# Attention into a top-1 mixture of experts: two comparisons in one piece, kept tokens' slots on GpSimd, eleven filler matmuls instead of twenty

## The chip, the cores and the metric

The kernel runs on one core of a Trainium2 chip. The metric is the device time of one execution in microseconds (us), median of three runs. The engines of the core are named as the profile names them: PE (TensorE matmuls; PEld are its weight loads), DVE (VectorE), ACT (ScalarE), POOL (GpSimd) and SP (SyncE, which here only issues DMAs). Each engine works through its own instructions in the order in which the program holds them, and waits for the others on semaphores.

## What is computed

Attention over 4 batches, 8 heads, 768 positions and a head size of 64, with 4 sink positions and a window of 128; its output, 3072 tokens of 512 numbers, goes into a layer of 8 experts. Each token goes to the expert of its largest logit, each expert keeps at most 80 tokens (those with the largest gate weight), and all other tokens give zero rows.

```python
scores = np.where(is_sink | in_window, scores / 8, -1e9)
a = softmax(scores); x = (a @ v) as (3072, 512)
logits = x @ w_gate                      # (3072, 8)
expert_idx = np.argmax(logits, axis=1); gate_w = softmax(logits)[chosen]
for e in range(8):
    tok = tokens of e; if len(tok) > 80: keep the 80 with the largest gate_w
    out[tok] = gate_w[tok, None] * (np.maximum(x[tok] @ w1[e], 0.0) @ w2[e])
```

## The kernel before

**Stages.** The 3072 tokens are 24 tiles of 128. The main loop goes through attention in 48 ticks (`scores`, `softmax`, `exps`, `transposes`, `weighted`, `keep_x`). Behind it, in the shadow of the following ticks, come the token rows (`rows_turn`, `rows_keep`, `rows_scale`, `rows_write`, which writes them to `x_rows` in DRAM), the gate (`gate_products` to `gate_keys`) and the ranking. After the loop a piece of code written out by hand ends attention for the last four tiles (`g0` = 20 to `i` = 23), and finishes the ranking. Then the selection (`rank`, `hot`, `pi`, `idx_in`) makes the list of token numbers per expert, and the expert stage gathers the tokens' rows from `x_rows` by these numbers (`gather`, an indirect DMA on POOL's queue), transposes them (`tokens`, the tile `px`) and runs two matrix products per expert (`ffn1`, `ffn2`).

**Ranking.** A token's key is a number that orders by expert and gate weight. Tile i's tokens are compared with all tokens before them: `rank_compare` runs on DVE over a row of all keys, `krow`, in pieces of up to `PIECE` = 768 columns. A piece that ends in tile i itself is a SCALAR_TENSOR_TENSOR with the table `ties` as a second tensor, any other one a TENSOR_SCALAR; both add up along the row. At tile `CUT` = 16 the first 2048 tokens are thinned to at most 80 per expert, so later tiles compare from column 2048 on (`C0`), and with the 640 kept keys (`kept_row`, piece number `NPC - 1`). Tiles 22 and 23 have 896 and 1024 columns of their own: two pieces each, 0 and 1. PE counts the results by column (`rank_count`, `rank_count_last`).

**Kept tokens.** `kept_rank` (80 x 8) is where the kept tokens stand after all, and `kept_hots` (80 x 8 x 80) their one-hot slots. DVE makes them in one TENSOR_TENSOR. PE multiplies them with `kept_picks` into `pi`, and behind that the `hot` of the last eight tiles with `picks`. ACT copies `lanes` out of `pi`, DVE makes `idxf`, POOL `idx_in`.

**Order.** From the loop to the end of the ranking the order on every engine is that of the code (`manual_schedule`). In the selection this holds for DVE and POOL, in the expert stage for all. SP issues weights (`load_weight`, 1 MB in four DMAs) and token rows in one queue, in program order.

**Fillers.** `warm(n)` issues n matmuls of no use on PE. Between the selection and the expert stage 20 more such matmuls (`warm1`, 480 columns each) stand on PE ahead of the first `tokens`.

Of the kernel before, what the change touches and what calls it, by code (L numbers as in the profile page):

```python
# [243 lines left out]
def attention_moe(ctx: ExitStack, tc, q, k, v, n_sink, window, w_gate, w1, w2, capacity, q_t, k_t, v_t, vs_t, wg_t, out):  # L244
# [28 lines left out]
    picks = const.tile([P, NTILE, 5, E], BF16, name="picks")  # L273
    PIECE, NPC, NGT = 768, 4, 6
    CUT = 16
# [52 lines left out]
    with ExitStack() as actx:  # L328
# [136 lines left out]
        po.memset(negc, NEG)  # L465
        ties = const.tile([P, PIECE], BF16, name="ties")
        e_down = const.tile([P, E], F32, name="e_down")
# [24 lines left out]
        def make_ties():  # L492
            po.memset(ties, TINY)
            po.affine_select(out=ties[:, PIECE - P:], in_=ties[:, PIECE - P:], pattern=[[-1, P]],
                             compare_op=ALU.is_gt, fill=0.0, base=0, channel_multiplier=1)
# [96 lines left out]
        def transposes(t):  # L592
            prob = st[(t, "p")]
            pp = ps_p.tile([P, 2, 2, P], F32, tag="pp", name=f"pp_{t}")
            for a in range(2):
                for h in range(2):
                    pe.transpose(pp[:, a, h], prob[:, a, h, SINK:], ident)  # L597
            st[(t, "pp")] = pp
# [5 lines left out]
        def sinks_keep(t):  # L604
            ac.copy(stt_rows[t % 2][0:SROWS].bitcast(F32R), ts_bank)
# [192 lines left out]
        def keys_keep(i0, nb):  # L798
            ac.copy(krow[:, i0 * P:(i0 + nb) * P], gst.pop((i0, "pk"))[:, 0:nb * P])
            for i in range(i0, i0 + nb):  # L800
                lo = 0 if i < CUT else C0
                todo = [(i, n, c, min(c + PIECE, (i + 1) * P)) for n, c in enumerate(range(lo, (i + 1) * P, PIECE))]
                if i >= CUT and i0 > CUT:
                    todo.append((i, NPC - 1, None, None))
                rank_todo.extend(todo)
            if i0 == CUT:
                rank_todo.extend((i, NPC - 1, None, None) for i in range(i0, i0 + nb))
# [3 lines left out]
        def rank_compare():  # L811
            i, n, c0, c1 = rank_todo.pop(0)
            gt = wk.tile([P, PIECE], BF16, tag="gt", name=f"gt_{i}_{n}", bufs=NGT)
            ra = parts[:, i, n:n + 1]
            if c0 is None:
                ve.tensor_scalar(gt[:, 0:E * CAP], kept_row, keys[:, i:i + 1], None, ALU.is_ge, ALU.add, accum_out=ra)
                rank_done.append((None, None, gt))
                return
            w = c1 - c0
            if c1 == (i + 1) * P:  # L820
                ve.scalar_tensor_tensor(gt[:, 0:w], krow[:, c0:c1], keys[:, i:i + 1], ties[:, PIECE - w:],
                                        ALU.subtract, ALU.is_gt, accum_out=ra)
            else:
                ve.tensor_scalar(gt[:, 0:w], krow[:, c0:c1], keys[:, i:i + 1], None, ALU.is_ge, ALU.add,
                                 accum_out=ra)
            if min(i * P, c1) > c0:
                rank_done.append((c0, min(i * P, c1), gt))
# [240 lines left out]
        with tc.manual_schedule():  # L1068
# [65 lines left out]
            sink_probs(t)  # L1134
            transposes(t)
            keep_probs(t)
            weighted(t - 1)
            keep_x(t - 1)
            rows_scale(g0, 0)
            rows_write(g0, 0, nc.sync)  # L1140
            own_probs(t)
            before_probs(t)
            assert not rank_todo, rank_todo
            recip(i, 1)
            keys_turn(g0, 2)
            keys_keep(g0, 2)
            sinks_turn(t)
            sinks_keep(t)
            compare(g0, NPC - 1)
# [12 lines left out]
            keep_x(t)  # L1162
            for _ in range(2):
                load_weight()
            rows_turn(g0, 1)
            gate_products(i, 1)
            rows_turn(i - 1, 0)
            rows_keep_scaled(g0, 1, "xr")
            rows_write(g0, 1, nc.sync)
            gate_logits(i, 1)  # L1170
            keys_turn(i - 1, 1)
# [16 lines left out]
            rank_count()  # L1188
            for n in (NPC - 1, 0, 1):
                compare(i - 1, n)  # L1190
# [20 lines left out]
            for c in range(E // 2):  # L1211
# [11 lines left out]
            kept_hots = const.tile([CAP, E, CAP], BF16, name="kept_hots")  # L1223
            ve.tensor_tensor(kept_hots, slot_row[0:CAP, None, :].to_broadcast([CAP, E, CAP]),
                             kept_rank[:, :, None].to_broadcast([CAP, E, CAP]), ALU.is_equal)
            in_row = {}
            for j in range(CUT, NTILE - 1):
                in_row.setdefault(j // NM, []).append(j % NM)
            for r, ms in in_row.items():
                j0, j1 = r * NM + ms[0], r * NM + ms[-1] + 1  # L1230
                ve.tensor_tensor(colacc[:, j0:j1], colacc[:, j0:j1],
                                 ct[:, 0:c0].rearrange("p (m k) -> p k m", k=rows)[:, r, ms[0]:ms[-1] + 1], ALU.subtract)
            warm(3)
            compare(i, 1)
            rank_count_last(more)
            warm(3)
# [3 lines left out]
    with ExitStack() as fctx:  # L1240
# [40 lines left out]
        with ExitStack() as wctx:  # L1281
            wps = wctx.enter_context(tc.tile_pool(name="ps_warm", bufs=1, space=PSUM))
            wt = wps.tile([P, 512], F32, name="warm1")
            for _ in range(20):
                pe.matmul(wt[0:CAP, 0:480], hot[:, NNEW - 1], hot[:, 0:6].rearrange("p t c -> p (t c)"), start=True, stop=True)
# [198 lines left out]
```

## Time and profile before

| | |
|---|---|
| median of three runs | 297.01 us (296.69 to 297.58) |
| profiled execution, its own time | 295.55 us |
| its span, first to last instruction | 293.8 us |
| busy: PE, DVE, ACT, POOL | 94%, 58%, 56%, 55% of the span |
| last tick's scores, start of the hand-written end | about 179 us |
| expert stage, first transpose to last matmul on PE | 206.3 to 287.9 us |
| mean granted TensorE clock | 0.983 |

A row of the timeline gives the start in us from the span's start, the duration in us (of the whole group where several equal instructions were merged, `x20`), the engine, the line of the kernel, the operation, what it writes and reads, the shapes, and in brackets the idle time of the engine ahead of it and who ended that wait. `SPq` is SP issuing a DMA. A table of stretches gives each engine's busy us, the granted clock (`PEclk`, 1.00 is 2.4 GHz and 0.50 is 1.2 GHz) and the DMA share.

### The profile page before, as it was taken

To read this page: it belongs to the slowest core of one execution; us is meant where nothing else is said; L and a number is where in the kernel's file an instruction comes from. 1 tells how busy PE (TensorE), PEld (TensorE's weight loads), DVE (VectorE), ACT (ScalarE), POOL (GpSimd) and SP (SyncE) were. 2 spreads that over 40 slices of the span, in tenths; PEclk is the share of its full clock that TensorE was granted. 3 is DMA by queue.
4 is the path that set the end of the run, shared out by engine and by line. 5 is a ranking of instruction groups with operands and counts; after the bars stand their busy time and mean duration, and the time that the engine had idled before them with its cause. 6 is when DMAs were issued, how large, how long until landed. Compare 5 with 4: busy or idle time off the path is not lost. (4 is left out here: it accounts for less than half of the span.)

```text
span 293.8 us, 10499 instructions
## 1 busy us (share of the span) xinstructions
PE 277.6 (94%) x4015; PEld 218.0 (74%) x4015; DVE 169.4 (58%) x564; ACT 165.1 (56%) x670; POOL 160.6 (55%) x365
## 2 busy tenths in 40 slices
PE   7989999999999999999999999988999999999991
PEld 2666777667777677777668777644999999999980
DVE  6678868767888979989996897990000000000001
ACT  4867888878887878687678778630112122212210
POOL 5966978658988768769757686735211121011111
PEclk9999999999999999999999999995999999999997
DMA  6989570899560999764174915595999999999501
GB/s 173 381 281 367 220 284 6 291 280 325 198 243 32 288 340 407 269 207 146 49 284 138 353 50 170 166 317 193 322 315 297 310 278 321 325 291 305 206 26 34
DMA packets 33364, 69.71 MB, mean 237 GB/s; under 512 B 4251, under 2 KB 6427, under 8 KB 32923
## 3 DMA queue, kind: packets, MB, share of 16 engines
q1 hardware_dynamic: 32282, 66.34, 66.6%
q0 software_dynamic: 1024, 2.62, 3.0%
q8 instruction: 34, 0.56, 0.8%
q14 instruction: 24, 0.19, 0.2%
HBM read 55.05 MB, written 13.89 MB: 235 GB/s over the span
## 5 line engine op out<-in xcount | busy, mean ns | idle before, releaser
L581 ACT ACTIVATE prob<-sc,nm 128x132 f32<-128x132 f32 (+1 forms) x192 | 68.9, 376 | 8.0 <-DVE nm L571 7.8
L544 PE MATMUL sc<-kv,q 64*128 64x260 f32 (+1 forms) x384 | 57.6, 401 | 5.1 <-ACT prob L581 3.7
L544 PEld LDWEIGHTS sc<-kv,q 64*128 64x128 f32 x384 | 30.1, 185 | 25.1 <-ACT prob L581 15.3
L609 ACT COPY pt<-pp 128x512 f32<-128x512 f32 x48 | 28.1, 585 | 32.4 <-PE pp L597 27.0
L571 DVE TENSOR_REDUCE nm<-sc 128x2 f32<-128x264 f32 (+1 forms) x96 | 41.3, 431 | 3.3
L564 DVE COPY_PREDICATED sc<-upper,sc 128x256 f32<-128x256 int8 x80 | 33.7, 422 | 15.8 <-PE sc L544 10.8
L581 ACT ACTIVATION_READ_ACCUMULATOR prob<-sc,nm 128x1 f32 x192 | 40.6, 211 | 0.0
L638 PE MATMUL xp<-pt,kv 128*64 128x128 f32 x384 | 37.0, 285 | 0.0
L1335 DVE COPY xs<-px 128x320 f32<-128x320 f32 x7 | 3.4, 491 | 56.3 <-PE px L1330 49.5
L617 POOL TENSOR_SCALAR_AFFINE_SELECT own<-pt 128x512 f32<-128x512 f32 (+1 forms) x48 | 27.2, 566 | 15.6 <-ACT pt L609 14.3
L1404 POOL DMA_INDIRECT out_dram<-y,idx x8 | 7.4, 925 | 46.1 <-ACT y L1398 42.0
L597 PEld LDWEIGHTS pp<-ident,prob 128*128 128x128 f32 x192 | 20.2, 141 | 15.9 <-issue 10.5
L597 PE MATMUL pp<-ident,prob 128*128 128x128 f32 x192 | 31.4, 286 | 0.0
L638 PE MATMUL xp<-own,kv 128*64 128x128 f32 x320 | 31.1, 273 | 0.0
L624 POOL TENSOR_SCALAR_AFFINE_SELECT pt<-pt 128x512 f32<-128x512 f32 (+1 forms) x48 | 28.3, 589 | 3.3
L688 POOL TENSOR_TENSOR xr<-xr,rs 128x512 f32<-128x512 f32 x21 | 22.4, 1067 | 6.7 <-ACT xr L676 6.4
L1352 PE MATMUL ph<-xs,w 128*64 128x80 f32 x640 | 25.6, 233 | 0.1
L1370 PE MATMUL py<-h,w 128*64 128x80 f32 x640 | 24.8, 234 | 0.6 <-ACT yt L1381 0.6
L1370 PEld LDWEIGHTS py<-h,w 128*64 128x64 f32 x640 | 23.1, 137 | 1.6 <-issue 0.8
L1352 PEld LDWEIGHTS ph<-xs,w 128*64 128x64 f32 x640 | 23.6, 137 | 0.4 <-DVE xs L1332 0.3
L638 PEld LDWEIGHTS xp<-pt,kv 128*64 128x64 f32 x384 | 21.1, 136 | 3.5 <-POOL pt L624 0.2
L1356 ACT ACTIVATE h<-ph 128x320 f32<-128x320 f32 x16 | 7.0, 437 | 29.3 <-PE ph L1352 29.3
(193 smaller groups left out, 523.0 us busy)
## 6 DMA issues: line engine op xcount, KB each, us to landing
w<-in_moe_w_dram SPq DMA_DIRECT2D x80, 256.0 KB, 4.7
kv_w<-in_moe_w_dram SPq DMA_DIRECT2D x48, 256.0 KB, 4.3
kv<-in_v_t_dram SPq DMA_DIRECT2D x12, 512.0 KB
out_dram<-zeros SPq DMA_DIRECT2D x24, 256.0 KB, 2.5
x_rows<-xr SPq DMA_DIRECT2D x24, 256.0 KB, 2.1
q<-in_q_t_dram SPq DMA_DIRECT2D x11, 512.0 KB, 5.7
kv<-in_k_t_dram SPq DMA_DIRECT2D x3, 1584.0 KB, 8.4
kv<-in_k_t_dram SPq DMA_DIRECT2D x2, 528.0 KB, 6.3
```

The lines of the kernel that those rows point to most:

```text
L544: pe.matmul(sc[:, h, c0:c0 + w], qs[g][r, hp, j % 2 * P:(j % 2 + 1) * P], ks[b][r, hp, k0:k0 + w], start=True, stop=True)
L564: ve.copy_predicated(own, upper, sc[:, :, 0:P])
L571: ve.tensor_reduce(out=nm, in_=sc[:, :, lo_c:hi_c], axis=AX.X, op=ALU.max, negate=True)
L581: ac.activation(prob[:, a, h, p0:], sc[:, h, lo_c:hi_c], AF.Exp, bias=nm[:, h:h + 1], scale=1.0, accum_out=ssum[:, n, 2 * hp + h:2 * hp + ...
L597: pe.transpose(pp[:, a, h], prob[:, a, h, SINK:], ident)
L609: ac.copy(pt, st.pop((t, "pp")))
L617: po.affine_select(out=own[:, a0:], in_=pt[:, a0:], pattern=[[0, 2 - a0], [0, 2], [1, P]], compare_op=ALU.is_ge, fill=0.0, base=0, channel ...
L624: po.affine_select(out=pt[:, a0:], in_=pt[:, a0:], pattern=[[0, 2 - a0], [0, 2], [-1, P]], compare_op=ALU.is_gt, fill=0.0, base=0, channel ...
L638: pe.matmul(xp[h * D:(h + 1) * D, a * P:(a + 1) * P], val[:, (2 * hp + h) * D:(2 * hp + h + 1) * D], pr[:, a, h], start=False, stop=(a == ...
L688: po.tensor_tensor(xr, xr, gst[(i0, "rs")][:, n, :, None].to_broadcast([P, H, D]), ALU.mult)
L1352: pe.matmul(ph[m * D:(m + 1) * D, f], columns(0, e, c, fc * P + m * D), x[:, c], start=(c == 0 and not (wide and f)), stop=(c == DC - 1), ...
L1370: pe.matmul(to[m * D:(m + 1) * D, dc], columns(1, e, k, dc * P + m * D), h[:, k], start=(k == 0), stop=(k == HC - 1), skip_group_check=True)
```

## The change

Six edits, all but the first in the hand-written end.

1. Pieces of tiles 16 and up may have 1024 columns (`WHOLE`): tiles 22 and 23 are compared in one SCALAR_TENSOR_TENSOR each. `ties` grows to 1024 columns, and two result tiles `gtw` are added. One `warm(3)` between the two old pieces of tile 23 goes.
2. `kept_hots` is made on POOL, in eight TENSOR_SCALARs of 80 x 80, one per expert.
3. For the last tick, POOL does the two selections of probabilities (`own_probs`, `before_probs`) ahead of scaling the rows of tile 20 (`rows_scale`), and the write of these rows follows later.
4. The transpose of the last tick's sink columns (`sinks_turn`) and its copy (`sinks_keep`) come earlier on PE and ACT.
5. Of two loads of weights in a row, the second is issued behind the write of tile 21's rows.
6. The 20 fillers ahead of the expert stage become 11.

```diff
-    PIECE, NPC, NGT = 768, 4, 6
+    PIECE, NPC, NGT, WHOLE = 768, 4, 6, 1024
...
-        ties = const.tile([P, PIECE], BF16, name="ties")
+        ties = const.tile([P, WHOLE], BF16, name="ties")
...
+                width = WHOLE if i >= CUT else PIECE
+                todo = [(i, n, c, min(c + width, (i + 1) * P)) for n, c in enumerate(range(lo, (i + 1) * P, width))]
...
-            gt = wk.tile([P, PIECE], BF16, tag="gt", name=f"gt_{i}_{n}", bufs=NGT)
+            if c0 is not None and c1 - c0 > PIECE:
+                gt = wk.tile([P, WHOLE], BF16, tag="gtw", name=f"gt_{i}_{n}", bufs=2)
+            else:
+                gt = wk.tile([P, PIECE], BF16, tag="gt", name=f"gt_{i}_{n}", bufs=NGT)
...
             transposes(t)
+            sinks_turn(t)
             keep_probs(t)
+            sinks_keep(t)
             weighted(t - 1)
             keep_x(t - 1)
+            own_probs(t)
+            before_probs(t)
             rows_scale(g0, 0)
             rows_write(g0, 0, nc.sync)
-            own_probs(t)
-            before_probs(t)
...
-            sinks_turn(t)
-            sinks_keep(t)
...
-            for _ in range(2):
-                load_weight()
+            load_weight()
             rows_turn(g0, 1)
             gate_products(i, 1)
             rows_turn(i - 1, 0)
             rows_keep_scaled(g0, 1, "xr")
             rows_write(g0, 1, nc.sync)
+            load_weight()
...
-            for n in (NPC - 1, 0, 1):
+            for n in (NPC - 1, 0):
                 compare(i - 1, n)
...
-            ve.tensor_tensor(kept_hots, slot_row[0:CAP, None, :].to_broadcast([CAP, E, CAP]),
-                             kept_rank[:, :, None].to_broadcast([CAP, E, CAP]), ALU.is_equal)
+            for e in range(E):
+                po.tensor_scalar(kept_hots[:, e], slot_row[0:CAP], kept_rank[:, e:e + 1], 1.0, ALU.is_equal, ALU.mult)
...
-            warm(3)
-            compare(i, 1)
-            rank_count_last(more)
             warm(3)
             ve.tensor_tensor(colacc[:, CUT:i], colacc[:, CUT:i], more[:, 0:i - CUT], ALU.subtract)
...
-            for _ in range(20):
+            for _ in range(11):
                 pe.matmul(wt[0:CAP, 0:480], hot[:, NNEW - 1], hot[:, 0:6].rearrange("p t c -> p (t c)"), start=True, stop=True)
```

DVE at the end of the ranking, before: the comparisons of tiles 22 (`gt_0_3434`, `gt_1_3436`) and 23 (`gt_0_3482`, `gt_1_3505`), the kept tokens' slots and the last `hot`.

```order
L824 TENSOR_SCALAR gt_0_3434,parts<-krow,keys 128x768
L821 SCALAR_TENSOR_TENSOR gt_1_3436,parts<-krow,keys,ties 128x128
L816 TENSOR_SCALAR gt_3_3463,parts<-kept_row,keys 128x640
L824 TENSOR_SCALAR gt_0_3482,parts<-krow,keys 128x768
L1216 TENSOR_REDUCE os<-ot 128x8
L1221 TENSOR_TENSOR kept_rank<-kept_rank,ct 80x8
L1222 TENSOR_TENSOR kept_rank<-kept_rank,last 80x8
L1224 TENSOR_TENSOR kept_hots<-slot_row,kept_rank 80x640
L1231 TENSOR_TENSOR parts<-parts,ct 128x2
...
L821 SCALAR_TENSOR_TENSOR gt_1_3505,parts<-krow,keys,ties 128x256
L1237 TENSOR_TENSOR parts<-parts,more 128x7
L1255 TENSOR_REDUCE rank<-parts 128x8
```

DVE at the same place, after the change:

```order
L825 SCALAR_TENSOR_TENSOR gt_0_3434,parts<-krow,keys,ties 128x896
L820 TENSOR_SCALAR gt_3_3461,parts<-kept_row,keys 128x640
L825 SCALAR_TENSOR_TENSOR gt_0_3480,parts<-krow,keys,ties 128x1024
L1220 TENSOR_REDUCE os<-ot 128x8
L1225 TENSOR_TENSOR kept_rank<-kept_rank,ct 80x8
L1226 TENSOR_TENSOR kept_rank<-kept_rank,last 80x8
L1235 TENSOR_TENSOR parts<-parts,ct 128x2
...
L1238 TENSOR_TENSOR parts<-parts,more 128x7
L1256 TENSOR_REDUCE rank<-parts 128x8
L1264 TENSOR_TENSOR hot<-slot_row,rank 128x320 x2
```

Two operations with one tensor became two with two tensors, the last piece of tile 23 moved ahead of `os`, and `kept_hots` left DVE.

POOL from the end of the ranking to the first gather, after the change (`off` and `ot` lead to `os` and `kept_rank`, `xg` takes the gathered rows); before, the row of `kept_hots` is not there and all others stand in the same order.

```order
L1203 TENSOR_TENSOR off<-off,kept_ahead 128x8
L1205 TENSOR_TENSOR ot<-onehot,off 128x64
L1207 TENSOR_TENSOR kept_rank<-kept_slot,off 80x8
L1221 TENSOR_TENSOR parts<-later,os 128x8
L1229 TENSOR_SCALAR kept_hots<-slot_row,kept_rank 80x80 x8
L1252 MEMSET xg_3529 1x1
...
L1276 TENSOR_SCALAR idx_in<-idxf 80x8
L1292 DMA xg_3529<-x_rows,idx_in 80x512
```

Eight instructions now stand between POOL's last sum and its making of the token numbers.

SP's queue over the last rows and weights, before:

```order
L692 DMA x_rows<-xr_0_3197 128x512
L317 DMA kv_w_3312<-in_moe_w_dram 128x512 x8
L692 DMA x_rows<-xr_1_3340 128x512
L692 DMA x_rows<-xr_0_3369 128x512
L692 DMA x_rows<-xr_0_3410 128x512
L317 DMA kv_w_3312<-in_moe_w_dram 128x512 x4
```

and after the change:

```order
L692 DMA x_rows<-xr_0_3197 128x512
L317 DMA kv_w_3312<-in_moe_w_dram 128x512 x4
L692 DMA x_rows<-xr_1_3336 128x512
L317 DMA kv_w_3312<-in_moe_w_dram 128x512 x4
L692 DMA x_rows<-xr_0_3369 128x512
L692 DMA x_rows<-xr_0_3410 128x512
L317 DMA kv_w_3312<-in_moe_w_dram 128x512 x4
```

Ahead of the last write of rows (`xr_0_3410`, tile 23) stand the same transfers as before; only tile 21's rows (`xr_1`) moved in between the weights.

## Rows read from the trace of the kernel before

**Rows 1.** Table of stretches: five engines' busy us, PEclk, DMA share, GB/s.

```profile
199.30:205.00 5.70, 5.69 (x15) 2.69 (x15) 0.00 (x0) 0.00 (x0) 3.82 (x8) 0.50 0.44 148
205.00:205.50 0.50, 0.50 (x4) 0.20 (x3) 0.00 (x0) 0.00 (x0) 0.00 (x0) 0.72 1.11 295
...
206.30:281.00 74.70, 74.07 (x1977) 71.66 (x1975) 3.68 (x8) 14.32 (x30) 10.39 (x11) 1.00 0.89 291
```

**Rows 2.** Timeline from the selection to the first transpose: start, duration, engine, what.

```profile
197.89 0.64 PE L1266 MATMUL pi<-picks,hot 128*80 128x40 bf16 x8
...
199.15 0.28 POOL L1275 TENSOR_SCALAR idx_in<-idxf 80x8 int32<-80x8 f32 x1 [3.00 <-DVE idxf L1274]
199.31 7.14 PE L1285 MATMUL warm<-hot 128*80 128x480 bf16 x20 [0.78 <-ACT tab L1278]
...
200.66 1.22 POOL L1291 DMA_INDIRECT xg<-x_rows,idx_in  x1 [1.23 <-DMA x_rows<-xr]
...
206.29 0.44 PE L1330 MATMUL px<-ident,xg 80*128 80x80 f32 x4
```

**Rows 3.** View of the tile xg, first gather alone: us from its start to landing.

```profile
DMA to landing us min/median/max: 3.3/3.3/3.3
```

**Rows 4.** View of x_rows, last write (tile 23) alone: durations, first and last start.

```profile
L692 SPq DMA_DIRECT2D x_rows<-xr x1: 319/319/319, 193.0 to 193.0; - x1
...
DMA to landing us min/median/max: 6.7/6.7/6.7
```

**Rows 5.** View of the tile w, the last six DMAs of weights.

```profile
L317 SPq DMA_DIRECT2D w<-in_moe_w_dram x6: 328/328/338, 268.9 to 273.0; - x6
...
DMA to landing us min/median/max: 4.5/4.5/4.5
```

**Rows 6.** Timeline of PE, start of the last expert's second product.

```profile
281.16 1.33 PE L1370 MATMUL py<-h,w 128*64 128x80 f32 x32 [0.58 <-ACT yt L1381]
```

**Rows 7.** Timeline of DVE at the end of the ranking.

```profile
193.49 1.01 DVE L824 TENSOR_SCALAR_CACHE_REDUCE gt<-krow,keys 128x768 bf16<-128x768 f32 x1
...
194.42 0.21 DVE L1216 TENSOR_REDUCE os<-ot 128x8 f32<-128x64 f32 x1
...
195.02 0.82 DVE L1224 TENSOR_TENSOR kept_hots<-slot_row,kept_rank 80x640 bf16<-80x640 f32 x1
...
195.96 0.47 DVE L821 SCALAR_TENSOR_TENSOR gt<-krow,keys,ties 128x256 bf16<-128x256 f32 x1
...
197.25 0.89 DVE L1263 TENSOR_TENSOR hot<-slot_row,rank 128x320 bf16<-128x320 f32 x2
```

**Rows 8.** Timeline of DVE and POOL: one POOL operation twice, beside different DVE operations.

```profile
186.22 0.88 DVE L821 SCALAR_TENSOR_TENSOR gt<-krow,keys,ties 128x640 bf16<-128x640 f32 x1
186.32 0.94 POOL L769 TENSOR_SCALAR picks<-onehot,lane 128x16 bf16<-128x16 f32 x1 [0.82 <-DVE ahead L765]
...
190.68 0.87 DVE L816 TENSOR_SCALAR_CACHE_REDUCE gt<-kept_row,keys 128x640 bf16<-128x640 f32 x1
...
190.78 0.28 POOL L769 TENSOR_SCALAR picks<-onehot,lane 128x16 bf16<-128x16 f32 x1 [0.93 <-DVE onehot L764]
```

**Rows 9.** Timeline of POOL: the sums for the kept tokens, and a wider TENSOR_SCALAR earlier.

```profile
85.72 0.32 POOL L769 TENSOR_SCALAR picks<-onehot,lane 128x64 bf16<-128x64 f32 x1
...
193.50 0.20 POOL L1199 TENSOR_TENSOR off<-off,kept_ahead 128x8 f32<-128x8 f32 x1 [0.49 <-ACT off L1196]
...
194.05 0.20 POOL L1203 TENSOR_TENSOR kept_rank<-kept_slot,off 80x8 f32<-80x8 f32 x1
```

**Rows 10.** Timeline of the last tick: POOL's row scaling and selection, PE, SP's weights.

```profile
183.16 1.04 POOL L688 TENSOR_TENSOR xr<-xr,rs 128x512 f32<-128x512 f32 x1 [0.61 <-ACT xr L676]
...
184.86 0.64 POOL L624 TENSOR_SCALAR_AFFINE_SELECT pt<-pt 128x512 f32<-128x512 f32 x1
...
185.55 0.44 PE L638 MATMUL xp<-pt,kv 128*64 128x128 f32 x4
...
186.69 4.25 SPq L317 DMA_DIRECT2D kv_w<-in_moe_w_dram  x8
```

More of the change, by code (lines that the diff above doesn't have):

```diff
@@ L493, in make_ties @@
             po.memset(ties, TINY)
-            po.affine_select(out=ties[:, PIECE - P:], in_=ties[:, PIECE - P:], pattern=[[-1, P]],
+            po.affine_select(out=ties[:, WHOLE - P:], in_=ties[:, WHOLE - P:], pattern=[[-1, P]],
                              compare_op=ALU.is_gt, fill=0.0, base=0, channel_multiplier=1)
@@ L801, in keys_keep @@
                 lo = 0 if i < CUT else C0
-                todo = [(i, n, c, min(c + PIECE, (i + 1) * P)) for n, c in enumerate(range(lo, (i + 1) * P, PIECE))]
+                width = WHOLE if i >= CUT else PIECE
+                todo = [(i, n, c, min(c + width, (i + 1) * P)) for n, c in enumerate(range(lo, (i + 1) * P, width))]
                 if i >= CUT and i0 > CUT:
@@ L820, in rank_compare @@
             if c1 == (i + 1) * P:
-                ve.scalar_tensor_tensor(gt[:, 0:w], krow[:, c0:c1], keys[:, i:i + 1], ties[:, PIECE - w:],
+                ve.scalar_tensor_tensor(gt[:, 0:w], krow[:, c0:c1], keys[:, i:i + 1], ties[:, WHOLE - w:],
                                         ALU.subtract, ALU.is_gt, accum_out=ra)
```

## The prediction

> **What bounds the kernel now.** I first read the table of stretches. From 206.3 to 281 us PE works without a break: 74.07 of 74.70 us, at the full clock [rows 1]. So the expert stage is as long as its matmuls, and a change ahead of it is worth what it does to the start of that stage, the first `px` at 206.29 [rows 2]. An earlier start reaches the end only if the weights keep ahead: the last are issued at 273.0 and six of that size took 4.5 us to land, so about 277.5, and the last expert's second product starts at 281.16 [rows 5, 6]. That is a lead of some 3.7 us; up to about 3 us of gain is not eaten by the transfers.
>
> Next I asked what `px` waits for. The timeline shows three things [rows 2]: the list `idx_in` ends at 199.43, the gather starts at 200.66 and is put down to the landing of `x_rows`, and `px` follows the last filler. The last write of rows is issued at 193.0 and lands 6.7 us later, at 199.7 [rows 4], so not the list but this write let the gather go, 0.94 us behind the landing. The gather lands 3.3 us after its start [rows 3], at 204.0. Yet `px` starts at 206.29, because PE is in its 20 fillers. They run from 199.31, at 0.50 of the clock until a little past 205.0 (the slice 205.0 to 205.5 has 0.72, a rise near 205.28) [rows 1]. At that clock one takes about 0.40 us (5.70 us for some 14), and at full clock 0.20. **The expert stage starts 2.2 us behind its data, because of fillers.**
>
> **The fillers.** Eleven from the same start would end at 199.31 + 11 x 0.40 = 203.7 at the low clock, ahead of the data at 204.0. If nothing else moved, `px` would start at 204.0 to 204.1, a gain of 2.2 us, less what a low clock costs the expert stage. The other edits decide when the fillers start and when the data come.
>
> **The two comparisons.** SCALAR_TENSOR_TENSOR takes 0.47 us at 256 columns and 0.88 at 640 [rows 7, 8], so 1.07 ns a column: an estimate of 0.33 for 128, 1.15 for 896 and 1.29 for 1024. A TENSOR_SCALAR of 768 holds DVE 0.93 us (193.49 to 194.42) [rows 7]. Tile 22 goes from 0.93 + 0.33 to 1.15, tile 23 from 0.93 + 0.47 to 1.29: 0.11 us less each. Taking `kept_hots` off DVE saves it another 0.82 [rows 7]. By DVE's own work, and with the round trip to PE between the two last pieces gone, the final `hot` would start at about 196.0 instead of 197.25.
>
> But a SCALAR_TENSOR_TENSOR is not free for POOL. One TENSOR_SCALAR on POOL took 0.94 us while DVE did one of 640 columns, and 0.28 beside a TENSOR_SCALAR with sums [rows 8]: POOL finished 0.16 us behind DVE's end at 187.10. The change puts such operations where TENSOR_SCALARs stood, and POOL's sums `off`, `ot` and `kept_rank` (193.50 to 194.25, [rows 9]) ran beside the one that becomes the 1024-column comparison (193.38 to 194.67 by the lengths above). I therefore put them behind it, together with the last of the gate's pieces, which the 896-column comparison held up in the same way: 194.7 + 0.2 + 0.75 = 195.65. DVE's `os` and two subtractions on `kept_rank` wait for them and took 0.6 together (194.42 to 195.02 [rows 7]), so `kept_rank` is ready near 196.2, against 195.0 before. If POOL were not held up it would be 194.67 + 0.6 = 195.3.
>
> **The slots on POOL.** The nearest row is POOL's TENSOR_SCALAR of 64 columns with a scalar per partition, 0.32 us [rows 9]; eight are 2.6 us, against 0.82 on DVE. From 196.2 that is 198.8. The final `hot`, 0.89 us of DVE with two tensors [rows 7], now falls beside them. If POOL slips one operation between its two halves, some 0.3 of it is lost; I take 199.1. Wholly unhindered (195.3 + 2.6) it is 197.9; wholly held up, 196.2 + 2.6 + 0.89 = 199.7. The Trainium skill has this as a rule that speaks against the edit: "SBUF — State Buffer", section "Who interferes with whom", says that a DVE instruction with two SBUF inputs contends with a GpSimd instruction that reads SBUF, over the port pair that they share, and that the lock is exclusive. The two rows of L769 agree with it for the comparison; that it also holds for `hot` is not seen in these rows. Without the rule the slots would end at 197.9, with the whole of it at 199.7.
>
> PE starts the eight `hot` matmuls at 197.89 now, 1.54 us ahead of the end of `idx_in` and 1.42 ahead of the fillers [rows 2]. Behind slots that end at 199.1 `idx_in` ends at 200.6 and the fillers start at 200.5, each 1.2 us later than before. **So this edit makes the chain longer, not shorter.** That costs less than it looks, since the gather had waited for `x_rows` anyway: it starts between 200.66 and 200.6 + 1.23 = 201.8 (1.23 being the idle time ahead of it now); I take 201.2. Then the data land at 204.5, the fillers end at 200.5 + 4.4 = 204.9, and `px` starts there: 1.4 us earlier than 206.29.
>
> **Rows and weights.** POOL's selections started behind a scaling of 1.04 us, and PE took `pt` at 185.55, right behind their end at 185.50 [rows 10]. They now start at most those 1.04 us earlier. But PE has the gate's products and the sink terms in between, and the early sink transpose costs it 0.1 ahead of them. I take 0, between -0.2 and +0.2. The scaled rows of tile 20 come as much later, by the 0.64 and its like, some 1 to 2 us behind 184.2, where the scaling ended; the weights behind them on SP were issued at 186.69, so nothing in the queue is held up by more than a little. The moved megabyte lets tile 21's rows go earlier, but the last write has the same transfers ahead of it: 0, with 0.3 us either way on its landing. The longer `ties` is a memset of 1024 instead of 768 columns early in attention, under POOL's idle time: 0. The `warm(3)` that goes filled a wait that goes too: 0.
>
> **The clock.** `px` at 204.9 would run at the low clock until it rises. If it rises at 205.28 again, 0.4 us run at half speed and 0.2 are lost; if it rises as long after the fillers' start as before (5.97 us, so 206.5), 0.8. I take 0.3.
>
> **Sum.** 1.4 - 0.3 = 1.1 us gained. The profiled execution took 295.55 us (a span of 293.8), which becomes 294.45; it was 1.46 below the median of the runs shown, and the same gain on that median gives **295.9 us**. What a measurement of this kernel can tell from no change is about 0.3%, 0.9 us: below 296.1 is faster, above 297.9 slower.
>
> **Rivals.**
> - *POOL is not held up.* The slots end at 197.9, ahead of `hot`'s end; the list comes as before, the gather at 200.66, the data at 204.0, the fillers end at 203.7 and `px` starts at 204.1, with 1.2 us at the low clock, 0.6 lost: 2.2 - 0.6 = 1.6, 295.4 us. For it: several POOL operations ran at their usual length beside TENSOR_SCALARs. Against it: the rows of L769. Chance 0.20.
> - *The gain of the fillers is used up by the longer chain.* The slots are held up for all of `hot` and end at 199.7, `idx_in` at 201.2, the gather starts 1.23 later at 202.4, the data land at 205.7: 0.6 earlier than 206.29, 0.1 lost to the clock, 296.5 us. The same comes out if the 20 fillers of the runs timed ended sooner than in the profile, which a sooner rise of the clock would do (at full clock they would end at 203.4). Chance 0.27.
> - *Slower: the fillers end too soon and the clock stays low.* If PE stands idle between the last filler and `px`, the work of the fillers may count for nothing, and the expert stage itself has to bring the clock up. The fillers needed 5.97 us for that (199.31 to 205.28); at half speed 3.0 us are lost. With `px` at 204.5 that is 207.5, 1.2 later than 206.29: 298.2 us. It decides if the data come clearly behind 200.5 + 4.4, or if the clock rises early, the fillers run at 0.20 and end 2 us sooner. Against it: in my times the fillers and the data meet within 0.4 us. Chance 0.11.
> - *The edits do nothing:* `px` follows the fillers, and nine fewer stand there; this I don't see.
>
> **How the numbers follow.** My case has 0.42; three quarters of it lie below 296.1. With the first rival, faster has 0.32 + 0.20 = 0.52. The rest of my case and the second rival give 0.37 within 0.3%, the third 0.11. The range goes from 294.9 (the first rival with no loss to the clock and 0.1 more from POOL) to 297.5 (the second rival with a write that lands 0.3 later and 0.8 lost to the clock); it leaves out the third.
>
> **What the profile after would show.** `px` near 204.9, right behind the fillers or the landing; the eight slots from about 196.2, ending behind `hot`, and PE's `hot` matmuls waiting for POOL, not DVE; `off`, `ot` and `kept_rank` on POOL behind the 1024-column comparison; the gather no longer waiting for `x_rows` but for `idx_in`; the expert stage as long as before, but for its first microsecond. I am wrong if the slots take far less than 0.3 us each, if the clock is still low at 207, or if PE waits for weights near the end.

## The result and the profile after

The changed kernel takes 299.67 us (median of 6 runs, 299.14 to 300.48) against 297.74 of the kernel before, measured beside it (6 runs, 296.69 to 298.32). The ratio is 1.0061, with a 95% interval of 1.0036 to 1.0087: **slower by 1.9 us**. Forecast were 295.9 us, 1.1 below the 297.01 of the runs then known, in a range of 294.9 to 297.5; the time lies outside it. The profiled execution took 299.14 us with a span of 297.4.

The table of stretches answers to [rows 1] (busy us of PE, PEld, DVE, ACT and POOL, then PEclk, DMA share and GB/s):

```profile
199.30:205.00 5.70, 3.76 (x17) 2.19 (x18) 1.43 (x5) 0.34 (x2) 2.61 (x7) 0.52 0.09 35
205.00:205.50 0.50, 0.50 (x3) 0.19 (x2) 0.00 (x0) 0.00 (x0) 0.38 (x1) 0.50 0.00 0
206.30:281.00 74.70, 73.34 (x1893) 69.94 (x1893) 3.68 (x8) 14.00 (x29) 11.28 (x15) 1.00 0.91 296
```

Two things have changed. Between 199.3 and 205 the DMA engines stand nearly still (a share of 0.09, where it was 0.44), since gathers and weights start later. And in the expert stage PE is no longer quite without a break (73.34 of 74.70 us, where it was 74.07). The timeline of the changed kernel (start, duration, engine, what, and in brackets the idle time before it and what ended it) shows where the first comes from; it answers to [rows 2, 7, 9]:

```profile
193.41 1.28 DVE L825 SCALAR_TENSOR_TENSOR gt<-krow,keys,ties 128x1024 bf16<-128x1024 f32 x1
...
194.73 0.20 POOL L1203 TENSOR_TENSOR off<-off,kept_ahead 128x8 f32<-128x8 f32 x1
...
195.71 0.16 DVE L1226 TENSOR_TENSOR kept_rank<-kept_rank,last 80x8 f32<-80x8 f32 x1
...
195.96 4.32 POOL L1229 TENSOR_SCALAR kept_hots<-slot_row,kept_rank 80x80 bf16<-80x80 f32 x8
196.17 0.17 DVE L1238 TENSOR_TENSOR parts<-parts,more 128x7 f32<-128x7 f32 x1
...
200.31 0.20 DVE L1256 TENSOR_REDUCE rank<-parts 128x8 f32<-128x48 f32 x1 [3.97 <-POOL kept_hots L1229]
...
200.55 0.89 DVE L1264 TENSOR_TENSOR hot<-slot_row,rank 128x320 bf16<-128x320 f32 x2
...
202.57 0.26 POOL L1276 TENSOR_SCALAR idx_in<-idxf 80x8 int32<-80x8 f32 x1 [2.08 <-DVE idxf L1275]
202.74 4.18 PE L1286 MATMUL warm<-hot 128*80 128x480 bf16 x11 [0.78 <-ACT tab L1279]
...
203.60 1.22 POOL L1292 DMA_INDIRECT xg<-x_rows,idx_in  x1 [0.77 <-POOL idx_in L1276]
...
207.04 0.47 PE L1331 MATMUL px<-ident,xg 80*128 80x80 f32 x4
```

The eight slots take 4.32 us, and `rank` on DVE stands idle for 3.97 us until the last of them ends, although the operand that it reads, `parts`, was done at 196.34 (L1238). So `hot` runs behind the slots, not beside them, `idx_in` ends at 202.83 instead of 199.43, the gather starts at 203.60 instead of 200.66, and `px` at 207.04 instead of 206.29. That is 0.75 us later; the span is 3.6 us longer. The rest lies behind `px`, and e11 and e12 below show whose it is. Against a second trace of the kernel before (e11, `px` at 203.98) it is 3.06 us later; the 1.9 us of the medians lie between the two.

### The profile page after: what moved, and what is told of

It reads as the page before. It is cut to its first block, busy times and chain, and to the rows that moved or that the text cites. A ratio compares the mean times of both kernels' runs of the same rounds, so it can differ in the third digit from the quotient of the medians.

```text
span 297.4 us, 10476 instructions
## 1 busy us (share of the span) xinstructions
PE 277.6 (93%) x4003; PEld 218.6 (74%) x4003; DVE 168.1 (57%) x559; ACT 165.1 (56%) x670; POOL 167.0 (56%) x373
## 3 DMA queue, kind: packets, MB, share of 16 engines
q0 software_dynamic: 1024, 2.62, 2.9%
## 5 line engine op out<-in xcount | busy, mean ns | idle before, releaser
L564 DVE COPY_PREDICATED sc<-upper,sc 128x256 f32<-128x256 int8 x80 | 33.8, 422 | 15.8 <-PE sc L544 10.7
L1371 PE MATMUL py<-h,w 128*64 128x80 f32 x640 | 26.1, 234 | 1.3 <-issue 0.7
L1353 PE MATMUL ph<-xs,w 128*64 128x80 f32 x640 | 26.9, 233 | 0.3 <-issue 0.2
L1371 PEld LDWEIGHTS py<-h,w 128*64 128x64 f32 x640 | 24.0, 137 | 2.9 <-issue 2.0
L1353 PEld LDWEIGHTS ph<-xs,w 128*64 128x64 f32 x640 | 24.8, 137 | 0.7 <-issue 0.3
```

The source lines that it names most:

```text
L564: ve.copy_predicated(own, upper, sc[:, :, 0:P])
L1353: pe.matmul(ph[m * D:(m + 1) * D, f], columns(0, e, c, fc * P + m * D), x[:, c], start=(c == 0 and not (wide and f)), stop=(c == DC - 1), ...
L1371: pe.matmul(to[m * D:(m + 1) * D, dc], columns(1, e, k, dc * P + m * D), h[:, k], start=(k == 0), stop=(k == HC - 1), skip_group_check=True)
```

## The experiments

My first theory (A) was that the slots on POOL cost the time, by their length and by `rank`'s wait for them. Its rivals were (B) that the eleven fillers cost it through the clock, (C) the other moves, and beside them the question whether the expert stage waits for weights that start late.

**The slots taken back (e1), and the slots alone (e2).** e1 is the changed kernel with one edit, e2 the kernel before with the opposite one:

```
e1:
-            for e in range(E):
-                po.tensor_scalar(kept_hots[:, e], slot_row[0:CAP], kept_rank[:, e:e + 1], 1.0, ALU.is_equal, ALU.mult)
+            ve.tensor_tensor(kept_hots, slot_row[0:CAP, None, :].to_broadcast([CAP, E, CAP]),
+                             kept_rank[:, :, None].to_broadcast([CAP, E, CAP]), ALU.is_equal)
e2: the same lines, + and - exchanged
```

> The changed kernel with kept_hots as one TENSOR_TENSOR on DVE again; the other edits stay. Theory A (the loss comes from the eight slot operations on POOL, 4.32 us, for whose end rank on DVE waits): rank starts near 197.0 instead of 200.31, idx_in ends near 199 instead of 202.83, the gather and the weights behind it start about 2.5 us earlier, PE has no idle stretch among the first five experts, and the time is about 2 us below the changed kernel's 299.7, near 297 to 297.7 or, if the 11 fillers bring anything, below that. Theory B (the loss comes from the eleven fillers, through the clock): the time stays near 299.5 and the clock rises later than the start of px. Theory C (the loss comes from the other moves, merged comparisons and order of the last tick): idx_in and the gather stay late although kept_hots takes 0.8 us.

> The kernel before with kept_hots alone moved to POOL, eight operations; 20 fillers and the rest stay. Theory A: the slots take about 0.53 us each again, rank starts when the last ends, near 195.0 + 4.3 = 199.4, idx_in ends near 202, the gather starts near 202.8, the first weight behind it near 205.3, and the 20 fillers, at the low clock, end after the data; the time is 300 us or more, 2 to 3 us over before. Theories B and C: no slower than before by more than 0.5 us.

e1 took 295.43 us against 296.55 of the kernel before beside it, a ratio of 0.9971 (0.9939 to 1.0004); e2 took 299.56, a ratio of 1.0101 (1.0056 to 1.0145). The timeline of e2:

```profile
195.52 4.61 POOL L1225 TENSOR_SCALAR kept_hots<-slot_row,kept_rank 80x80 bf16<-80x80 f32 x8 [0.16 <-DVE kept_rank L1222]
...
200.17 0.20 DVE L1255 TENSOR_REDUCE rank<-parts 128x8 f32<-128x48 f32 x1 [3.70 <-POOL kept_hots L1225]
...
202.42 0.26 POOL L1275 TENSOR_SCALAR idx_in<-idxf 80x8 int32<-80x8 f32 x1 [2.08 <-DVE idxf L1274]
202.59 6.03 PE L1285 MATMUL warm<-hot 128*80 128x480 bf16 x20 [0.79 <-ACT tab L1278]
203.45 1.22 POOL L1291 DMA_INDIRECT xg<-x_rows,idx_in  x1 [0.77 <-POOL idx_in L1275]
...
208.45 0.44 PE L1330 MATMUL px<-ident,xg 80*128 80x80 f32 x4
```

and that of e1:

```profile
197.68 0.20 DVE L1256 TENSOR_REDUCE rank<-parts 128x8 f32<-128x48 f32 x1
...
199.94 0.28 POOL L1276 TENSOR_SCALAR idx_in<-idxf 80x8 int32<-80x8 f32 x1 [2.56 <-DVE idxf L1275]
...
205.04 0.47 PE L1331 MATMUL px<-ident,xg 80*128 80x80 f32 x4 [0.58 <-DMA xg<-x_rows,idx_in]
```

The slots alone bring a loss of the size of the whole one (the two intervals overlap), and without them the change is no slower than before. That settles A against B and C. One number missed: I expected `idx_in` near 199 in e1, and it ended at 200.22, later than before. The other moves don't make the list earlier (e7, e9).

**What one slot costs (e6).** The changed kernel with 24 more operations on POOL behind the slots, while DVE waits, so that nothing contends with the groups shown below:

```
+            for _ in range(4):
+                po.tensor_scalar(pb[0:CAP, 0, 0], slot_row[0:CAP], kept_rank[:, 0:1], 1.0, ALU.mult, ALU.mult)
...
+            for _ in range(4):
+                po.tensor_scalar(pb[0:CAP, 0, 3, 0:16], slot_row[0:CAP, 0:16], kept_rank[:, 0:1], 1.0, ALU.is_equal, ALU.mult)
...
```

> The changed kernel with 24 more operations on POOL behind the eight slots, four of each form, which write memory that nobody reads, while DVE waits: the slot's form with mult in place of is_equal; with an f32 result; with 64 columns and mult; with 40 and 16 columns and is_equal; with a constant in place of the scalar per partition. The time itself says nothing; it is longer by what the operations take. My pricing took 0.32 us from a row of 64 columns with mult. If the comparison is what costs, the forms with mult take about 0.33 and those with is_equal 0.53 or a width's share of it. If the columns cost (0.28 for 16 columns and 0.32 for 64 being the floor of the issue rather than a slope), 80 columns take 0.53 with mult too, and 64 about 0.45. If the bf16 result costs, the f32 form is shorter.

The groups of POOL by form (busy us, mean ns of one, idle us before):

```profile
L1229 POOL TENSOR_SCALAR kept_hots<-slot_row,kept_rank 80x80 bf16<-80x80 f32 x8 | 4.3, 556 | 0.1
L1235 POOL TENSOR_SCALAR probe_f<-slot_row,kept_rank 80x80 f32<-80x80 f32 x4 | 2.2, 552 | 0.3
...
L1239 POOL TENSOR_SCALAR probe_bf<-slot_row,kept_rank 80x40 bf16<-80x40 f32 x4 | 1.7, 418 | 0.3
L1241 POOL TENSOR_SCALAR probe_bf<-slot_row,kept_rank 80x16 bf16<-80x16 f32 x4 | 1.4, 342 | 0.3
L1233 POOL TENSOR_SCALAR probe_bf<-slot_row,kept_rank 80x80 bf16<-80x80 f32 x4 | 1.3, 327 | 0.3
L1237 POOL TENSOR_SCALAR probe_bf<-slot_row,kept_rank 80x64 bf16<-80x64 f32 x4 | 1.3, 313 | 0.3
```

L1233 and L1229 differ only in `mult` for `is_equal`: 327 against 556 ns. With `mult`, 16 more columns cost 14 ns; with `is_equal`, 64 more cost 210 (342 to 552), 3.3 ns a column. The type of the result changes nothing (552 in f32). So the comparison is what costs, and the row of 64 columns from which I had priced the slot was a multiplication.

**Why `rank` waits (e4).** `rank` reads nothing of the slots. It and `hot` lie in a pool opened where the ranking's tiles lay, and of those the slots read `kept_rank`. e4 gives both memory of their own:

```
-            rank = sm.tile([P, NNEW], F32, name="rank")
+            rank = const.tile([P, NNEW], F32, name="rank")
-            hot = sm.tile([P, NNEW, CAP], BF16, name="hot")
+            hot = const.tile([P, NNEW, CAP], BF16, name="hot")
```

> The changed kernel with rank and hot in memory of their own (the pool of constants) instead of the pool that is opened where the ranking's tiles lay; the slots stay on POOL. Theory A with the wait as one for memory: rank starts near 196.4, right behind the last subtraction on parts, and hot beside the slots; the list is then bound by the slots and eight matmuls behind them, idx_in ends 0.7 to 1 us earlier than 202.83, and the time is 0.5 to 1 us below the changed kernel. If the wait of rank is one for the order of the data, it stays at 200.3 and nothing changes. Beside that: if hot (two tensors on DVE) and the slots on POOL hold each other up, one of them is longer by some 0.5 us than in the changed kernel (hot 0.89, slots 0.53 each); if not, both keep their lengths.

The timeline of e4, and under it the view of L1229 (min/median/max ns of one):

```profile
196.03 4.64 POOL L1229 TENSOR_SCALAR kept_hots<-slot_row,kept_rank 80x80 bf16<-80x80 f32 x8
196.51 0.20 DVE L1256 TENSOR_REDUCE rank<-parts 128x8 f32<-128x48 f32 x1
...
196.75 0.92 DVE L1264 TENSOR_TENSOR hot<-slot_row,rank 128x320 bf16<-128x320 f32 x2
...
202.13 0.26 POOL L1276 TENSOR_SCALAR idx_in<-idxf 80x8 int32<-80x8 f32 x1 [1.25 <-DVE idxf L1275]
...
206.60 0.47 PE L1331 MATMUL px<-ident,xg 80*128 80x80 f32 x4 [0.24 <-DMA xg<-x_rows,idx_in]
```

```profile
L1229 POOL TENSOR_SCALAR kept_hots<-slot_row,kept_rank x8: 549/552/867, 196.0 to 200.1; 80x80 bf16<-80x80 f32 x8
```

The wait is gone: `rank` starts at 196.51, 3.8 us earlier. It was a wait for memory, for the last reader of an old tile in its place (by the code `kept_rank`; that it was this one is not shown). And now `hot` runs beside the slots, which shows the price of that: one slot took 867 ns instead of 552, 0.32 us more, and `hot` 0.92 instead of 0.89. The rule that I had weighed (the Trainium skill, "SBUF — State Buffer", section "Who interferes with whom") says that the two contend. The trace agrees for one slot and 0.3 us; `hot` ran beside a second slot too, and that one kept its length (0.56 us), so POOL was not held up for all of `hot`. The list ends only 0.44 us earlier (202.39), less than the 0.7 to 1 that I expected, since the slots, 0.3 us longer, still end at 200.7 and PE's matmuls stand behind them. So it is mostly the slots' length that makes the list late; without the wait it is 0.44 us earlier. In time e4 had 298.92 us, a ratio of 1.0113 (1.0058 to 1.0168); whether its gain of 0.44 us reaches the end can't be read from runs that spread from 296.5 to 301.6; the trace is that of the fastest of them.

**The fillers alone (e3), four of them (e10), and the kernel before once more (e11).**

```
e3:
-            for _ in range(20):
+            for _ in range(11):
e10:
-            for _ in range(20):
+            for _ in range(4):
e11: no edit
```

> The kernel before with 11 fillers instead of 20, nothing else. What my prediction said: px starts at the landing of the first rows, near 204.1 instead of 206.29. Theory A with weights that just keep pace (the first weight behind the gathers is issued at 203.26 in the kernel before and does not move): px starts 2 us earlier, but PE waits for weights within the first experts and the end moves by less than 0.5 us: 297.2 to 297.9. If the weights have the 3.7 us of lead that I read at the end of the stream: 296. Theory B: slower, 298.5 or more, with the clock low after px has begun.

> The kernel before with 4 fillers instead of 20, nothing else. My slower rival, measured alone: the fillers end some 2.7 us ahead of the data (199.8 + 4 x 0.40 = 201.4 against 204.1), PE stands idle, and the clock is still low in the expert stage. If that stretch has to bring the clock up again, px starts at 204.1 as with 11 fillers, but the granted clock is 0.5 for 3 to 6 us behind it, 1.5 to 3 us are lost, and the time is 1 to 2 us over that of 11 fillers (295.8). If the fillers had no part in the clock, it is the same as with 11.

> The kernel before once more, for its trace: how far the end of its 20 fillers, and with it px, moves from one execution to another. In the first profile the clock rose at 205.28 and px started at 206.29. If the rise comes at another time, the fillers end and px starts earlier or later by as much as half of that. And whether its expert stage again has no stretch in which PE waits for nothing that the profile shows (87.5 us from px to the end), or is 88 to 90 us, as in most of the other kernels.

The timeline of e3:

```profile
199.83 4.50 PE L1285 MATMUL warm<-hot 128*80 128x480 bf16 x11 [0.78 <-ACT tab L1278]
200.69 1.22 POOL L1291 DMA_INDIRECT xg<-x_rows,idx_in  x1 [0.75 <-POOL idx_in L1275]
...
204.17 0.44 PE L1330 MATMUL px<-ident,xg 80*128 80x80 f32 x4
```

That is what I had forecast for this edit: `px` near 204.1, and in this execution, the fastest of 14, the span is 291.7 instead of 293.8, so all 2.1 us reach the end. Yet the median was only 295.80 against 296.55, a ratio of 0.9976 (0.9949 to 1.0004). The timeline of e11, the unchanged kernel, shows one reason; under it is its table of stretches:

```profile
199.72 4.21 PE L1285 MATMUL warm<-hot 128*80 128x480 bf16 x20 [0.78 <-ACT tab L1278]
200.58 1.22 POOL L1291 DMA_INDIRECT xg<-x_rows,idx_in  x1 [0.75 <-POOL idx_in L1275]
...
203.98 0.47 PE L1330 MATMUL px<-ident,xg 80*128 80x80 f32 x4
```

```profile
199.70:204.00 4.30, 4.23 (x21) 2.27 (x20) 0.00 (x0) 0.00 (x0) 3.03 (x5) 1.00 0.46 150
206.30:281.00 74.70, 73.46 (x1930) 70.57 (x1924) 3.44 (x7) 13.85 (x29) 9.53 (x11) 1.00 0.90 289
```

Here the clock is at 1.00 (2.4 GHz) through the fillers. Twenty of them take 4.21 us instead of 7.14, end with the data, and `px` starts at 203.98, 2.3 us earlier than in the profile that I had. In such an execution nine fewer fillers bring nothing. It is one of four traces with 20 fillers: in the first profile `px` stands 2.3 us behind the landing of its rows [rows 2, 3], in e2 1.8 us (the gather at 203.45 landed 3.2 us later), and in e7 some 1.5, an estimate from its gather at 201.21 and the 3.3 of [rows 3]. The mean granted clock says the same as far as a mean can: 0.983 in the first profile, 0.993 in e11, and 0.991 or more in 22 of the 63 runs of the kernel before that stand beside the experiments. So the fillers stood in the way more often than not, and e3's median gain of 0.7 us is a part of the 2.2; what takes the rest isn't shown. e10 shows the other side: with `px` at 204.35, the second `px` comes 4.24 us behind the first (208.59), against 2.94 in e3, since the clock is still low. The tables of stretches from the first to the second `px`, e10 and then e3 (PEclk is third from the end):

```profile
204.30:208.60 4.30, 4.25 (x69) 4.01 (x69) 0.24 (x1) 0.36 (x1) 1.86 (x5) 0.62 0.93 284
```

```profile
204.10:207.10 3.00, 2.87 (x69) 2.62 (x68) 0.24 (x1) 0.36 (x1) 1.78 (x5) 0.99 0.96 299
```

Too few fillers cost 1.3 us in this trace; e10 took 298.24 us, a ratio of 1.0031 (1.0006 to 1.0055), 0.55% over e3.

**The weights not held (e5, e8).** The weights behind the first gathers are held: a memset of one element on POOL, behind a gather in POOL's order, has to be done before SP issues them. e5 is the changed kernel, e8 that with `kept_hots` on DVE as in e1, both with

```
-                load_weight(hold=True)
+                load_weight()
```

> The changed kernel with the weights behind the gathers no longer held by a one-element memset on POOL; they are issued as soon as SP comes to them, near 197, into memory that is free. Slots, fillers and order as in the changed kernel. If the late start of the weights (206.20 in the changed kernel, 203.26 before) is what lengthens the expert stage there, the idle stretches of PE at 214.7, 230.8 and 241.8 are gone, px to the end takes 87.5 us as before instead of 90.4, and the time is 2 us or more below the changed kernel's, near 297.5. If the weights and the gathers then share the DMA engines to the loss of the gathers, the first rows land later than 3.2 us behind their issue, px moves by as much, and the time is no better than 299. If the expert stage is longer for another reason than the start of the weights, its idle stretches stay.

> The changed kernel with kept_hots on DVE again and the weights behind the gathers not held. Against the kernel with kept_hots on DVE alone (295.43 us, ratio 0.9971 to before): if the weights' start bounds the expert stage, PE has no idle stretch in it and the time falls by another 1 to 2 us, to 293.5 to 294.5; if they take the DMA engines from the gathers and from the last rows written, the first rows land later and the time is the same or worse.

Both became slower: 303.48 us, a ratio of 1.0151 (1.0122 to 1.0180), and 300.69, 1.0071 (1.0044 to 1.0097). The timeline of e5, the view of its first three gathers (two of them have a landing in the trace), and a row of its table of stretches:

```profile
200.68 0.80 SPq L317 DMA_DIRECT2D w<-in_moe_w_dram  x2
...
203.84 1.22 POOL L1292 DMA_INDIRECT xg<-x_rows,idx_in  x1 [0.77 <-DMA w<-in_moe_w_dram]
...
211.06 0.77 PE L1331 MATMUL px<-ident,xg 80*128 80x80 f32 x4 [4.20 <-DMA xg<-x_rows,idx_in]
```

```profile
DMA to landing us min/median/max: 7.1/7.2/7.4
```

```profile
211.00:216.30 5.30, 5.24 (x69) 4.92 (x70) 0.24 (x1) 0.36 (x1) 0.98 (x1) 0.50 1.04 287
```

With weights in flight a gather lands 7.2 us behind its issue instead of 3.3 [rows 3], PE stands idle for 4.2 us, and the second `px` comes 5.16 us behind the first, at a granted clock of 0.50; that adds 2.2 us to the 2.94 of e3. PE's pauses of some 0.4 us in the second products of the second and third expert (at 236.5 and 247.4) stayed, although the weights there were issued 30 us earlier and more. So the late start of the weights doesn't cause these pauses.

**The merged comparisons alone (e7), and the order of the last tick with eleven fillers (e9).** e7 is the kernel before with the change's lines on `WHOLE`, `ties`, `gtw` and the loop over pieces; e9 has its lines on the last tick and the 11 fillers.

```
e7:
-            for n in (NPC - 1, 0, 1):
+            for n in (NPC - 1, 0):
...
-            warm(3)
-            compare(i, 1)
-            rank_count_last(more)
e9:
+            own_probs(t)
+            before_probs(t)
             rows_scale(g0, 0)
             rows_write(g0, 0, nc.sync)
-            own_probs(t)
-            before_probs(t)
...
-            for _ in range(20):
+            for _ in range(11):
```

> The kernel before with the comparisons of tiles 22 and 23 in one piece each, alone; kept_hots on DVE, 20 fillers, the order of the last tick as before. My prediction said that the final hot, without kept_hots on DVE, would start 1.2 us earlier; with kept_hots still there the same steps (0.22 us saved on DVE, the round trip to PE between the two last pieces gone, POOL's three sums behind the 1024-column comparison) give a start of hot between 0.4 us earlier and 0.4 later than before, against the first expert selection of its tick. In the end nothing moves: idx_in stands ahead of the landing of x_rows by 0.3 us, and px follows the 20 fillers; within 0.3% of before.

> The kernel before with 11 fillers and the changed order of the last tick (probabilities' selections ahead of the row scaling, sink terms earlier, one weight behind the rows); comparisons in pieces as before, kept_hots on DVE. By the theory that the time follows the start of px alone: with the fillers alone (ratio 0.9976) px was at 204.17, bound by the list and the landing of x_rows; if the order brings the ranking earlier, px comes 0.2 to 0.5 us earlier than that and the ratio is 0.995 to 0.997; if it does not, 0.9975 as with the fillers alone.

e7: 298.76 against 298.34 us, a ratio of 1.0010 (0.9988 to 1.0033). e9: 297.03 against 297.22, 0.9997 (0.9970 to 1.0023). The timeline of e7:

```profile
195.10 0.20 POOL L1203 TENSOR_TENSOR off<-off,kept_ahead 128x8 f32<-128x8 f32 x1
...
196.28 0.82 DVE L1228 TENSOR_TENSOR kept_hots<-slot_row,kept_rank 80x640 bf16<-80x640 f32 x1
197.71 0.20 DVE L1256 TENSOR_REDUCE rank<-parts 128x8 f32<-128x48 f32 x1
...
200.13 5.99 PE L1286 MATMUL warm<-hot 128*80 128x480 bf16 x20 [0.78 <-ACT tab L1279]
201.21 1.22 POOL L1292 DMA_INDIRECT xg<-x_rows,idx_in  x1 [0.96 <-DMA x_rows<-xr]
...
205.96 0.44 PE L1331 MATMUL px<-ident,xg 80*128 80x80 f32 x4
```

Neither edit moves the time. In e7 POOL's `off` comes behind the 1024-column comparison (193.79 + 1.28 = 195.07), and `rank` starts at 197.71, against 197.01 and 197.42 in the two traces of the kernel before: the merge gives back what it saves, and some more. In e9 `rank` is at 197.29 and `px` at 204.38, as with the fillers alone.

**The changed kernel once more (e12).** No edit.

> The changed kernel once more, for its trace. The list, the gather and px should stand where they stood (idx_in ending at 202.8, gather 203.6, px 207.0, each within 0.5 us), as they follow from the slots. Open is the 90.4 us from px to the end, 2.9 more than before: if its idle stretches at 230.8 and 241.8 come again in the same two second products, they belong to the program; if they come elsewhere or not at all, they are a matter of the single execution.

Everything up to `px` came again: slots from 195.99 for 4.31 us, `idx_in` ending at 202.85, the gather at 203.62, `px` at 207.00. Its time was 298.54 us, and that of e11 beside it 295.78. The expert stage took 89.8 us (296.8 less 207.00). The waits of PE between 206 and 283 (us in total, times, longest), e12 and then e11:

```profile
PE py L1371 <- issue: 0.7, 2, 0.3
```

```profile
PE py L1370 <- issue: 0.7, 2, 0.3
...
PE ph L1352 <- issue: 0.2, 1, 0.2
```

From `px` to the end it is 87.5 us in the first profile of the kernel before (293.8 less 206.29) and in e3, but 90.1 in e11, 89.8 in e12 and 90.4 in the first profile of the changed kernel. Of the fourteen traces nine have the pauses in the second products of the second and third expert, three (e1, e2, e4) elsewhere, and two none: the profile that I argued from, and e3. **So the 2.9 us behind `px` come with the execution, not with the change: the unchanged kernel has 2.6 of them in e11, and e1, e7 and e9, without the slots on POOL, have 90.0 to 90.4 us as well.**

The kernels beside each other, with the start of `px` in the trace (one execution each, the ratio from all runs):

| kernel | `px`, us | ratio to before (95%) |
|---|---|---|
| before (two traces) | 206.29, 203.98 | 1 |
| e3, 11 fillers | 204.17 | 0.9976 (0.9949 to 1.0004) |
| e9, order and 11 fillers | 204.38 | 0.9997 (0.9970 to 1.0023) |
| e1, all but the slots | 205.04 | 0.9971 (0.9939 to 1.0004) |
| e7, merged comparisons | 205.96 | 1.0010 (0.9988 to 1.0033) |
| changed (two traces) | 207.04, 207.00 | 1.0061 (1.0036 to 1.0087) |
| e8, no slots, no hold | 207.99 | 1.0071 (1.0044 to 1.0097) |
| e2, slots alone | 208.45 | 1.0101 (1.0056 to 1.0145) |
| e5, changed, no hold | 211.06 | 1.0151 (1.0122 to 1.0180) |

By and large the time follows the start of the expert stage. e10 (204.35) stands above its place because of the clock, e4 (206.60) for no reason that its trace, of the fastest run, shows. No version is clearly faster than the kernel before.

## Why the prediction was wrong, point by point

Two steps failed. The larger is the price of the slots on POOL: forecast at 2.6 us beside `hot`, with a list 1.2 us later than before. They took 4.32 us, `rank` waited for their end, and the list came 3.4 us later (202.83 against 199.43); alone they cost 1.0% (e2). The smaller is the gain of the fillers, forecast at 2.2 us for that edit by itself and measured at 0.24%, 0.7 us, with an interval that takes in 0 (e3). The forecast had the sign of the slots right and their size too small for the gain that it set against them.

- **The expert stage as long as its matmuls, and a change ahead of it worth what it does to the first `px`**: the second half is right by and large, by the table above. The first held for the profile that I read (87.5 us); in e11 the same kernel has pauses and takes 90.1.
- **"The expert stage starts 2.2 us behind its data, because of fillers"**: true of the execution that I had, and too much for the kernel. e3's trace shows the gain in full, but in e2 and e7 `px` stands only 1.8 and some 1.5 us behind its data, and in e11 the clock was high, the fillers ended with the data, and there was nothing to gain. The rows showed that the fillers ran at 0.50 of the clock; I took that for a property of the kernel. The sentence in my second rival ("at full clock they would end at 203.4") had the other case, without the weight that it deserved.
- **"eight are 2.6 us"**: mis-sized, and the step that cost most; they took 4.32. The row that I priced from was nearest in shape but did another arithmetic: 0.33 us with `mult`, 0.55 with `is_equal` (e6). My upper bound took in contention, but not a dearer operation.
- **The final `hot` beside the slots**: wrong. `rank` waited for the slots to end, for memory, which e4 takes away; that alone brings the list back by 0.44 us. With the length and the wait, `idx_in` ended at 202.83 instead of my 200.6, the gather started at 203.60 instead of 201.2, and `px` at 207.04 instead of 204.9. My worst bound of this chain (slots ending at 199.7, gather at 202.4) fell short by 0.6 and 1.2 us.
- **POOL held up by the comparison**: right. I put `off` behind 194.7 and it started at 194.73; `kept_rank` was ready at 195.87, where I had 196.2. **Held up by `hot`**: a loss of some 0.3 us was right in size (0.32 in e4), though in the changed kernel the two never met.
- **The comparisons' lengths**, estimated at 1.15 and 1.29 us, took 1.15 and 1.28. That `hot` starts near 196.0 without `kept_hots` on DVE missed by 0.75 (196.75 in e4).
- **Rows, weights, `ties`, the order of the tick at 0**: right within what can be measured (e9). **Weights that keep ahead**: no run shows PE waiting for them.
- **The clock, 0.3 us lost**: nothing was lost, since `px` came later than the rise. **The third rival's mechanism** is real (e10), at 1.3 us instead of the 3.0 that I had worked out from one rise, but isn't what made this kernel slower.
- **The direction**: "so this edit makes the chain longer, not shorter" was right, and I still let the fillers outweigh it. Of my three signs of being wrong none came: the one on the slots looked only for cheaper ones.

## What to carry to other kernels

Price an operation by a row with the same arithmetic on the same engine, not only the same shape: on POOL a comparison cost 3.3 ns for each further column, and a multiplication 0.9 (e6). When work is moved to another engine, look for whoever takes over the memory of what it reads: a wait that one engine's own order made free becomes a wait between engines. And before a gain is built on one profile, ask which of its numbers hang on the clock of that execution: the same 20 fillers took 7.14, 6.03, 5.99 and 4.21 us in four traces, and what `px` waited for them went from 2.3 us to nothing.

## What the runs showed of the hardware that I had not expected

- The granted clock in the stretch ahead of the expert stage differs between executions of one program: 0.50 from 199.3 to 205.0 in the first profile of the kernel before, 1.00 from 199.7 to 204.0 in e11, where the program had given PE the same work before it.
- In nine of the fourteen traces PE pauses in the second products of the second and third expert, 0.1 to 0.4 us at a time, without a wait that the profile names ("issue"); the interval from one `px` to the next is then 10.7 to 11.0 us there, instead of 9.9. Weights aren't the reason: those that are used there had been issued 45 us earlier and more in e5. The Trainium skill, "Runtime: NRT & Kernel Launch", section "Instruction fetch mechanics", says that an engine's instructions come in blocks over a DMA queue of its own and that crossing into the next block is mostly hidden; no run here shows whether the pauses are such crossings. Their cause stays open.
- Gathers that share the DMA engines with weights land 7.1 and 7.4 us behind their issue instead of 3.3 (two of the first three in e5).
